# Chunk-selected attention with a gated projection on one core: half-head PSUM tiles joined to two-bank groups, one relu for both query parts, a new written order

## The chip, the cores and the metric

The kernel runs on one core of a Trainium2 chip. The metric is the device time of one execution in microseconds (us), given as the median of three runs.

## The reference, cut to what matters

There are 4 batches of 8 heads, 768 positions of 64 channels. Keys are cut into 24 chunks of 32. For every query an upper bound of each chunk's score is made from the chunk's smallest and largest key, the best 6 chunks that are not in the future are kept, and softmax attention runs over those. The result goes through a causal convolution of 5 taps, which gives a gate, and through two 512x512 projections.

```python
k_min = np.min(k_chunks, axis=3)
k_max = np.max(k_chunks, axis=3)
ub = np.sum(np.maximum(q[:, :, :, None, :] * k_min[:, :, None, :, :],
                       q[:, :, :, None, :] * k_max[:, :, None, :, :]), axis=-1)
ub = np.where(causal, ub, -1000000000.0)
top_chunks = np.argsort(ub, axis=-1)[..., -top_k:]
...
scores = np.where(mask, scale * np.matmul(q, k.transpose(0, 1, 3, 2)), -1000000000.0)
attn = softmax(scores)
x = np.matmul(attn, v)                       # heads side by side: 4 x 768 x 512
gate = 1.0 / (1.0 + np.exp(-causal_conv5(x, conv_w)))
return (gate * (x @ w_val)) @ w_out
```

## The kernel before

The 32 heads are worked as 16 pairs, 0 to 15, four pairs to a batch. `build` makes a graph of some 1500 operations, each with its engine, and `emit_in_order` writes them to the engines' queues in the order of a long list of names, `ORDER`; each engine then runs its own queue strictly in that order and waits by semaphores. So the list is what sets the order of the work, on each engine by itself. A name is an operation, a pair and a part: `E6.04` is the exponential of pair 6, head 0, score bank 4.

One pair goes through these steps:
- SP loads keys, queries and values (`Lk`, `Lq`, `Lv`). PE turns the two heads' keys into two PSUM banks (`KT`, line 649, 12 small transposes) and the queries likewise (`QT`). A bank holds, for both heads, one half of each 128-position block.
- DVE takes the largest and smallest key of each chunk, two reduces per bank, so four of 128x384 for a pair (`KX`, line 674). ACT copies the keys to fp16, one copy per bank (`KE`, line 663). POOL makes of the chunk bounds a high and a low fp16 part (`KB`, `KS`, lines 682 to 699).
- The queries, times 16, are split in the same way. ACT writes the high part QH, one copy per bank (`QH`, line 703). DVE writes the low part QL = 16 q - QH (`QL`, line 743, two of 128x320), the relu of the high part RH (`RH`, line 750, one of 128x640 fp16 from and to SBUF) and RL, the low part where q is positive and zero elsewhere (`RL`, line 756, two of 128x320: a compare of q, still in PSUM, times QL). It cannot be a relu of QL, since QH is rounded to nearest and QL can have either sign.
- PE sums the bounds with six matmuls per 128 queries (`BD`, line 784), DVE takes the 6th largest (`T8`, line 792) and marks the chunks below it (`CM`, line 799). For pairs 4 to 15 a transposing DMA on SP's queue turns the marks (`MD`).
- PE makes the scores in six groups of banks (`S`, lines 827 to 832), each group one bank for head 0 and one for head 1; the mask is added by a second matmul. A matmul of one head uses 64 of the array's rows, and those of the two heads run side by side. ACT takes the exponential, one instruction per head and bank, 128x512 or 128x128 (`E`, line 836). POOL zeroes the triangle on the diagonal (`A`, line 847). PE multiplies with the values (`AV`, line 856), DVE divides by the sum (`RC`, `NR`, lines 862 to 878).
- Per batch: the convolution as small matmuls for two pairs (`CV`, line 950) and as four multiply-adds on DVE for the other two (`TP`, line 936, "taps"), the tanh (`TH`), the value projection (`VL`, lines 964 and 971), its product with the gate, two of 128x384 per 128 channels (`GV`, line 976, DVE), the output projection (`OU`, line 984), its copy (`OE`) and the store (`ST`).

Pair 0 is handled apart, in two halves and with fp32 bounds, to start early. PE runs 36 filler matmuls (`F`, `G`, line 1002) at the start.

PSUM has 8 banks. Each group of the graph takes one bank when its first operation is written, the one that has been free for longest, and gives it back with its last:

```python
        for g in o.groups:
            if g.bank is None:
                g.bank = free.pop(0)
```

Two engines never read or write one bank at the same time: the copy on ACT and the reduces on DVE out of one bank wait for each other.

## Time and profile before

| | before |
|---|---|
| median of three runs | 175.83 us (174.57 to 175.96) |
| the profiled execution | 174.37 us, of which the span is 172.6 us and 1.77 us lie around it |
| busy in the span | PE 161.6, DVE 153.6, ACT 145.2, POOL 97.4 us |
| instructions | PE 3118 matmuls, DVE 464, ACT 320, POOL 218 |
| granted TensorE clock | 1.00 |
| first and last matmul | start 1.11 us, end 169.1 us |

In the tables of groups, "mean ns" is one instruction from its start to its end; where instructions of an engine follow each other without a pause they overlap by some tens of ns, and the chain of work gives the smaller time from one start to the next. PE's matmuls are pipelined and their ends are modelled, so that PE seems busy where it runs slowly; its real need is counted by starts.

### The profile page before, as it was taken

How to read it: one execution, taken by the hardware profiler on the slowest of the kernel's cores; microseconds unless marked ns; L12 is line 12 of the kernel's file. 1: busy time of each engine (PE TensorE's matmuls, PEld its weight loads, DVE VectorE, ACT ScalarE, POOL GpSimd, SP SyncE). 2: the span in 40 equal slices, each digit the busy share in tenths (PEclk: the TensorE clock that was granted, in tenths of full speed). 3: DMA queues.
4: the chain of work that ended last, by engine and by line, in shares of the span. 5: the costliest groups of instructions: out<-in, count | busy, mean ns of one | idle time of the engine just before them, and what ended most of it. 6: DMA issues, size and time to landing. Idle time of an engine off the chain costs nothing.

```text
span 172.6 us, 7674 instructions
## 1 busy us (share of the span) xinstructions
PE 161.6 (94%) x3118; PEld 107.8 (62%) x3118; DVE 153.6 (89%) x464; ACT 145.2 (84%) x320; POOL 97.4 (56%) x218
## 2 busy tenths in 40 slices
PE   7999999999878969999999999999999999999991
PEld 5675748776566745746764758656775646665541
DVE  0799999999999999999999999997299999669970
ACT  2387999999979988999999979797999979957441
POOL 7838489945999697186733916365718456500000
PEclk9999999999999999999999999999999999999999
DMA  4999999935999999968999979976959990334546
GB/s 95 224 240 261 235 234 251 237 75 97 193 148 220 148 211 201 213 153 198 185 183 157 237 188 217 197 158 148 233 104 238 249 217 0 66 91 181 189 187 239
DMA packets 98578, 31.50 MB, mean 182 GB/s; under 512 B 94187, under 2 KB 95467, under 8 KB 98544
## 3 DMA queue, kind: packets, MB, share of 16 engines
q1 hardware_dynamic: 97424, 29.96, 78.6%
q0 software_dynamic: 1120, 1.06, 4.2%
q8 instruction: 24, 0.39, 1.0%
q14 instruction: 10, 0.08, 0.2%
HBM read 20.98 MB, written 6.29 MB: 158 GB/s over the span
## 4 chain that ended last, share of the span: by engine, by line
PE 65%; DVE 21%; ACT 7%; POOL 2%; DMA 2%; issue 1%; DVEq 0%; POOLq 0%
PE ps L984 12%; PE ps L856 9%; PE ps L829 7%; PE ps L832 6%; PE ps L971 6%; PE ps L964 6%; ACT P L836 5%; DVE KK L674 5%; DVE G L936 5%; PE ps L649 5%; PE ps L950 4%; PE ps L784 4%; PE ps L1002 3%; DVE TOP L792 2%; DMA QM<-NS 2%; DVE QL L743 2%
## 5 line engine op out<-in xcount | busy, mean ns | idle before, releaser
L836 ACT ACTIVATE P<-ps 128x512 f16<-128x512 f32 (+1 forms) x192 | 89.6, 582 | 5.9 <-PE ps L832 5.5
L847 POOL TENSOR_SCALAR_AFFINE_SELECT P<-P 128x256 f16<-128x256 f16 (+1 forms) x64 | 37.2, 595 | 19.8 <-ACT P L836 18.4
L832 PE MATMUL ps<-QM,EM 64*128 64x512 f16 (+4 forms) x256 | 37.2, 290 | 0.7 <-DMA QM<-NS 0.4
L936 DVE SCALAR_TENSOR_TENSOR G<-xT,cwT,G 128x768 f32<-128x768 f16 x32 | 36.2, 1149 | 0.1
L674 DVE TENSOR_REDUCE KK<-ps 128x12 f32<-128x384 f32 x64 | 32.0, 546 | 4.7 <-PE ps L641 4.4
L829 PE MATMUL ps<-QH,KE 64*128 64x512 f16 (+4 forms) x256 | 35.6, 292 | 0.4 <-ACT P L836 0.4
L856 PEld LDWEIGHTS <-P 128*128 128x128 f16 x672 | 24.2, 97 | 9.0 <-issue 4.7
L856 PE MATMUL ps<-VA,P 128*128 128x65 f16 x672 | 27.5, 194 | 1.4 <-POOL P L847 1.4
L984 PE MATMUL ps<-wo,GV 128*128 128x512 f16 (+1 forms) x100 | 23.1, 371 | 0.0
L829 PEld LDWEIGHTS <-KE 64*128 64x128 f16 x256 | 13.7, 94 | 7.0 <-issue 1.4
L663 ACT ACTIVATE KE<-ps 128x384 f16<-128x384 f32 x32 | 16.1, 541 | 0.9 <-DVE KK L674 0.9
L992 ACT ACTIVATE OSB<-ps 128x512 f32<-128x512 f32 (+1 forms) x22 | 13.0, 616 | 4.3 <-PE ps L984 4.2
L976 DVE SCALAR_TENSOR_TENSOR GV<-G,ps 128x384 f16<-128x384 f32 x32 | 16.1, 542 | 0.0
L703 ACT ACTIVATE QH<-ps 128x384 f16<-128x384 f32 x32 | 15.3, 531 | 0.8 <-PE ps L829 0.6
L792 DVE MAX8 TOP<-ps 128x8 f32<-128x20 f32 (+4 forms) x160 | 15.6, 160 | 0.2
L768 POOL CAST VA<-vn 128x768 f16<-128x768 f32 x16 | 13.9, 869 | 3.2 <-DMA vn<-in_v_dram 3.1
L984 PEld LDWEIGHTS <-GV 128*128 128x128 f16 x100 | 8.7, 98 | 9.7 <-DVE GV L976 1.0
L743 DVE SCALAR_TENSOR_TENSOR QL<-ps,QH 128x320 f16<-128x320 f32 x30 | 13.8, 477 | 0.6 <-ACT QH L703 0.6
L832 PEld LDWEIGHTS <-EM 64*128 64x128 f16 x256 | 12.2, 94 | 3.4 <-issue 2.4
L756 DVE SCALAR_TENSOR_TENSOR RL<-ps,QL 128x320 f16<-128x320 f32 x30 | 13.8, 476 | 0.0
L971 PE MATMUL ps<-xT,wv 64*128 64x384 f16 x128 | 13.2, 323 | 0.4 <-DVE GV L976 0.4
L682 POOL TENSOR_TENSOR KK<-KK 128x24 f32<-128x24 f32 x15 | 3.7, 245 | 17.0 <-DVE KK L674 16.8
(87 smaller groups left out, 314.6 us busy)
## 6 DMA issues: line engine op xcount, KB each, us to landing
vn<-in_v_dram SPq DMA_DIRECT2D x16, 384.0 KB, 5.0
out_dram<-OSB SPq DMA_DIRECT2D x23, 256.0 KB, 3.4
kn<-in_k_dram SPq DMA_DIRECT2D x30, 192.0 KB, 3.9
qn<-in_q_dram SPq DMA_DIRECT2D x30, 192.0 KB, 4.1
wo<-in_moe_w_out_dram POOLq DMA_DIRECT2D x4, 128.0 KB, 4.5
kn<-in_k_dram SPq DMA_DIRECT2D x4, 96.0 KB, 2.5
qn<-in_q_dram SPq DMA_DIRECT2D x4, 96.0 KB, 2.8
wv<-in_moe_w_val_dram POOLq DMA_DIRECT2D x4, 64.0 KB, 3.7
```

What stands on the lines that cost most here:

```text
L663: nc.scalar.activation(out=spread(KE[p % 3], p, w), in_=bank(gr, None), func=AF.Copy)
L674: nc.vector.tensor_reduce(out=o, in_=i, axis=AX.X, op=ALU.min if mx else ALU.max)
L743: nc.vector.scalar_tensor_tensor(out=spread(QL[p % 2], p, w), in0=bank(gr, None)[:, 1:NT], scalar=QS, in1=spread(QH[p % 3], p, w)[:, 1:NT] ...
L792: nc.vector.max(out=TOP[p % 2][:, it - 1, s, :], in_=bank(gr, None)[:, it - 1, s * NCH:s * NCH + n])
L829: nc.tensor.matmul(out=pq[hh][:, col + a:col + n], lhsT=KE[p % 3][HP[hh], ks], rhs=QH[p % 3][HP[hh], q0 + a:q0 + n], start=True, stop=False)
L832: nc.tensor.matmul(out=pq[hh][:, col + a:col + n], lhsT=EM[HP[hh], ks], rhs=qm[HP[hh], q0 + a - 128:q0 + n - 128], start=False, stop=True)
L836: e.EX = lambda p, hh, bi, tot, gr: nc.scalar.activation(out=PT[hh, bi, p % 2][:, 0:tot], in_=bank(gr, None)[:, 0:tot], func=AF.Exp, scale ...
L847: nc.gpsimd.affine_select(out=ap, in_=ap, pattern=[[0, 2], [0, n], [1, 128]], compare_op=ALU.is_ge, fill=0.0, base=0, channel_multiplier=-1)
L856: nc.tensor.matmul(out=pav[:, qt, :], lhsT=PT[a, bi, p % 2][:, col:col + 128], rhs=VA[p % 3][:, hh, jt, :], start=(jt == 0), stop=(jt == qt))
L936: en.scalar_tensor_tensor(out=GT[sl], in0=x, scalar=w, in1=GT[sl], op0=ALU.mult, op1=ALU.add)
L971: nc.tensor.matmul(out=pv[h], lhsT=wval_sb[HP[h], gi, ws], rhs=xT[HP[h], (b % 2) * 2, gi, :, LD:LD + 128], start=(gi == 0), stop=False)
L984: nc.tensor.matmul(out=po[:, 0:z - a], lhsT=GVT[(b % 2) * NCT + et][:, s * 128:(s + 1) * 128], rhs=wout_sb[:, et, a:z], start=(et == 0), s ...
```

## The change

Four things are changed.

**Query parts.** The high part is scaled by `QD`, a little less than 16, so that its rounded value is never larger in size than 16 q; what is left, QL, then has the sign of q. High and low part lie side by side in one tile `QHL` (three of them, where QL had two buffers), and one relu of 128x1280 gives RH and RL together. The two `RL` of each pair are gone; the relu now stands behind both `QL`. The exponential's scale is divided by `QD` in place of 16.

**Two-bank groups.** A group may take two neighbouring banks (an even one and the next). The turned keys and queries, the scores of both heads, the convolution of both halves and the value projection each take such a pair of banks, and one instruction reads both: `KE`, `QH` and two `KX` per pair of heads in place of two, two and four; one `E` per score group in place of two (128x1024 or 128x256); `TH` and `GV` once per 768 columns in batches 0 to 2. In batch 3 `TH` and `GV` stay in halves. All of PSUM is one tensor of 8 banks; single banks are taken where the neighbour is already in use, if there is one.

**Nothing of PE's work changes**: the same 3118 matmuls with the same shapes.

**Written order.** `ORDER` is another list throughout.

```diff
+def take(free, size):
+    if size == 1:
+        b = next((x for x in free if x ^ 1 not in free), free[0])
+        free.remove(b)
+        return b
+    pairs = [x for x in free if x % 2 == 0 and x + 1 in free]
+    b = min(pairs, key=lambda x: max(free.index(x), free.index(x + 1)))
...
 ORDER = """
-Lk0.1 mfz F5 F14 F11 G6 mKB0 F13 cwl G11 G7 F7 F8 Lk0.0 F9 F6 ident identh G19 G2 G12 G15 KT0.1
...
+wval00 mfz F3 G12 F5 G13 G11 wval11 F12 cwl F1 F4 F2 mNS0 F15 ident mKB0 identh F6 G0 ident2 G3
...
+QD = QS * (1.0 - 2.0 ** -11)
...
-            grs = [g.group(), g.group()]
+            grs = [g.group(2)]
...
+            g.op("ACT", c, l, f"E{p}.{bi}", lambda gr=grs[0], bi=bi, tot=tot: e.EX(p, bi, tot, gr),
+                 [("sps", p, bi, hh) for hh in range(2)], keys, grs)
...
-    QH = [ct_([128, S], F16, f"QH{i}") for i in range(3)]
-    QL = [ct_([128, SELT * 128], F16, f"QL{i}") for i in range(2)]
-    RH = [ct_([128, SELT * 128], F16, f"RH{i}") for i in range(2)]
-    RL = [ct_([128, SELT * 128], F16, f"RL{i}") for i in range(2)]
+    QHL = [ct_([128, S + SELT * 128], F16, f"QHL{i}") for i in range(3)]
+    QH, QL = [x[:, 0:S] for x in QHL], [x[:, S:] for x in QHL]
+    RHL = [ct_([128, 2 * SELT * 128], F16, f"RHL{i}") for i in range(2)]
+    RH, RL = [x[:, 0:SELT * 128] for x in RHL], [x[:, SELT * 128:] for x in RHL]
...
     def RHv(p):
-        nc.vector.tensor_scalar(out=RH[p % 2], in0=QH[p % 3][:, 128:S], scalar1=0.0, scalar2=None,
+        nc.vector.tensor_scalar(out=RHL[p % 2], in0=QHL[p % 3][:, 128:], scalar1=0.0, scalar2=None,
                                 op0=ALU.max)
-    def RLv(p, w, gr):
-        nc.vector.scalar_tensor_tensor(out=spread(RL[p % 2], p, w), in0=bank(gr, None)[:, 1:NT],
-                                       scalar=0.0, in1=spread(QL[p % 2], p, w), op0=ALU.is_gt,
-                                       op1=ALU.mult)
...
-    e.EX = lambda p, hh, bi, tot, gr: nc.scalar.activation(
-        out=PT[hh, bi, p % 2][:, 0:tot], in_=bank(gr, None)[:, 0:tot], func=AF.Exp,
-        scale=0.125 / QS)
+    e.EX = lambda p, bi, tot, gr: nc.scalar.activation(
+        out=PT2[bi, p % 2][:, :, 0:tot], in_=bank(gr, None)[:, :, 0:tot], func=AF.Exp,
+        scale=0.125 / QD)
```

How the instructions stand on the engines' queues, at the three places of which the prediction speaks. The first is DVE, from the first query parts to the first marks after them. Before (`TENSOR_REDUCE` is `KX`, `COPY QM` the copy of the turned marks of pair 0, `MAX` is `T8`):

```order
L743 SCALAR_TENSOR_TENSOR QL_100<-ps_345,QH_99 128x5x64 [waits Activation_49]
L813 COPY QM_90<-ps_377 128x640 [waits PE_49]
L743 SCALAR_TENSOR_TENSOR QL_100<-ps_344,QH_99 128x5x64 [waits Activation_49]
L750 TENSOR_SCALAR RH_102<-QH_99 128x640
L756 SCALAR_TENSOR_TENSOR RL_104<-ps_345,QL_100 128x5x64 [waits DVE_49]
L743 SCALAR_TENSOR_TENSOR QL_101<-ps_389,QH_98 128x5x64 [waits Activation_49]
L750 TENSOR_SCALAR RH_103<-QH_98 128x640 [waits Activation_49]
L743 SCALAR_TENSOR_TENSOR QL_101<-ps_390,QH_98 128x5x64 [waits PE_49]
L756 SCALAR_TENSOR_TENSOR RL_104<-ps_344,QL_100 128x5x64 [waits DVE_49]
L756 SCALAR_TENSOR_TENSOR RL_105<-ps_390,QL_101 128x5x64 [waits DVE_49]
L756 SCALAR_TENSOR_TENSOR RL_105<-ps_389,QL_101 128x5x64
L674 TENSOR_REDUCE KK_109<-ps_457 128x6x2 [waits PE_49,Pool_49]
```

And in the changed kernel:

```order
L832 COPY QM_90<-psall 128x640 [waits PE_49]
L769 SCALAR_TENSOR_TENSOR QHL_99<-psall,QHL_99 128x5x64 [waits Activation_49]
L769 SCALAR_TENSOR_TENSOR QHL_99<-psall,QHL_99 128x5x64
L769 SCALAR_TENSOR_TENSOR QHL_98<-psall,QHL_98 128x5x64 [waits Activation_49]
L769 SCALAR_TENSOR_TENSOR QHL_98<-psall,QHL_98 128x5x64
L776 TENSOR_SCALAR RHL_101<-QHL_98 128x1280 [waits DVE_49]
L700 TENSOR_REDUCE KK_105<-psall 128x2x6x2 [waits PE_49,Activation_49,Pool_49]
L811 MAX TOP_113<-psall 128x8 [waits PE_49,Activation_49]
```

From the first `QL` to the next `KX` there were eleven instructions and are now five: the four `RL` are gone, the copy of the marks has moved ahead, and one of the two relus has moved behind that `KX` and the marks after it. The second place is ACT, from the end of pair 0's score groups to the second group of pair 1, with `KE` and `QH` of pair 3 in between. Before:

```order
L836 ACTIVATE P_0_121<-ps_516 128x512 [waits PE_49]
L836 ACTIVATE P_0_121<-ps_517 128x512 [waits PE_49]
L663 ACTIVATE KE_87<-ps_457 128x6x64 [waits DVE_49,Activation_49]
L703 ACTIVATE QH_97<-ps_561 128x6x64 [waits PE_49]
L703 ACTIVATE QH_97<-ps_562 128x6x64 [waits PE_49]
L663 ACTIVATE KE_87<-ps_456 128x6x64 [waits DVE_49]
L836 ACTIVATE P_1_131<-ps_606 128x128 [waits PE_49]
L836 ACTIVATE P_1_131<-ps_605 128x128
L836 ACTIVATE P_1_130<-ps_611 128x512 [waits PE_49]
L836 ACTIVATE P_1_130<-ps_612 128x512 [waits PE_49]
```

And in the changed kernel:

```order
L856 ACTIVATE P_0_116<-psall 128x1024 [waits PE_49]
L689 ACTIVATE KE_87<-psall 128x2x6x64 [waits DVE_49,PE_49,Activation_49]
L856 ACTIVATE P_0_118<-psall 128x1024 [waits PE_49]
L729 ACTIVATE QHL_97<-psall 128x2x6x64 [waits PE_49,Activation_49]
L856 ACTIVATE P_1_127<-psall 128x256 [waits PE_49]
L856 ACTIVATE P_1_123<-psall 128x1024 [waits PE_49]
```

Each two instructions on neighbouring tiles have become one of twice the size, and `KE` and `QH` stand between whole score groups. The third place is the start of POOL's queue. Before:

```order
L1015 MEMSET KB_114 128x192
L1065 DMA cwl<-in_moe_conv_w_dram 5x512
L1022 MEMSET ident 128x128
L1018 ISA
L1018 AFFINE_SELECT ident<-ident 128x128 [waits Pool_49]
```

And in the changed kernel:

```order
L1107 DMA wv_66<-in_moe_w_val_dram 32x2x512 x2
L1092 DMA cwl<-in_moe_conv_w_dram 5x512
L1042 MEMSET NS_114 128x640
L1049 MEMSET ident 128x128
L1045 ISA
L1045 AFFINE_SELECT ident<-ident 128x128 [waits Pool_49]
```

The identity matrix, without which PE's first transposes cannot run, now stands behind two weight loads and a longer memset; the memset of `KB` has moved behind it.

More of the change, by code (lines that the diff above doesn't have):

```diff
@@ L85, in emit_in_order @@
             if g.bank is None:
-                g.bank = free.pop(0)
+                g.bank = take(free, g.size)
         o.emit()
@@ L90, in emit_in_order @@
             if g.left == 0:
-                free.append(g.bank)
+                free.extend(range(g.bank, g.bank + g.size))
+def take(free, size):
[5 more added lines that the diff above has]
+    b = min(pairs, key=lambda x: max(free.index(x), free.index(x + 1)))
+    free.remove(b)
+    free.remove(b + 1)
+    return b
 PARAMS = {
@@ L209 @@
+OE3.5 ST3.5 OU3.5z OU3.1 OE3.1 OE3.5z ST3.5z ST3.1
 """.split()
@@ L310, in turn @@
                      [grs[w]])
-        kgr = [g.group(), g.group()]
+        kgr = [g.group(2)] if halves else [g.group(), g.group()]
         turn("KT", "kn", "kps", kgr, e.KT)
-        for w in range(2):
+        if halves:
+            c, l = act(S)
+            kp = [("kps", p, w) for w in range(2)]
+            g.op("ACT", c, l, f"KE{p}", lambda: e.KEv(p, None, kgr[0]), kp,
+                 [("KE", k3, w) for w in range(2)], kgr)
+            for mx in range(2):
+                c, l = dve(S)
+                g.op("DVE", c, l, f"KX{p}.{mx}", lambda mx=mx: e.KX(p, None, mx, kgr[0]), kp,
+                     [("kk", k2, mx, w) for w in range(2)], kgr)
+        for w in range(0 if halves else 2):
             gr = kgr[w]
@@ L475, in pair @@
                  [("xh", xs)], ())
-            grs = {(h, r): g.group() for h in range(2) for r in range(2)}
+            grs = {r: g.group(2) for r in range(2)}
             for a in range(2):
@@ L494, in pair @@
             for et in range(NCT):
-                grs = [g.group() for _ in range(2)]
+                grs = [g.group(2)]
                 for a, z in ((0, 1), (1, 2)):
@@ L645, in turn @@
         t = (kn if src == "kn" else qn)[p % 4]
-        po = [bank(gr, [128, NT, 64]) for gr in grs]
+        po = bank(grs[0], [128, 2, NT, 64])
         for i in range(NT):
             for h in range(2):
-                nc.tensor.transpose(out=po[h][:, i, :], in_=t[HP[h], i, :],
+                nc.tensor.transpose(out=po[:, h, i, :], in_=t[HP[h], i, :],
                                     identity=ident[HP[h], HP[h]], tile_position=(64 * h, 0))
@@ L742, in QLv @@
     def QLv(p, w, gr):
-        nc.vector.scalar_tensor_tensor(out=spread(QL[p % 2], p, w), in0=bank(gr, None)[:, 1:NT],
+        nc.vector.scalar_tensor_tensor(out=spread(QL[p % 3], p, w), in0=bank(gr, None)[:, w, 1:NT],
                                        scalar=QS, in1=spread(QH[p % 3], p, w)[:, 1:NT],
@@ L818, in SC @@
     def SC(p, bi, grs):
-        pq = [bank(gr, [128, 512]) for gr in grs]
+        pb = bank(grs[0], [128, 2, 512])
+        pq = [pb[:, hh] for hh in range(2)]
         qm = QM[p % 3].rearrange("p i c -> p (i c)")
@@ L943, in CV @@
         x = xT[:, (p // 2) % 4]
-        pc = [bank(grs[h, r], [128, HB]) for h in range(2) for r in range(2)]
+        pb = [bank(grs[r], [128, 2, HB]) for r in range(2)]
+        pc = [pb[r][:, h] for h in range(2) for r in range(2)]
         for j in range(part * KSZ, part * KSZ + KSZ):
@@ L954, with cut @@
     e.CV = CV
+    def cut(t, h):
+        return t.rearrange("p (x c) -> p x c", x=2) if h is None else t[:, h * HB:(h + 1) * HB]
     e.TH = lambda sl, h, gr: nc.scalar.activation(
-        out=GT[sl][:, h * HB:(h + 1) * HB], in_=bank(gr, None), func=AF.Tanh, scale=0.5)
+        out=cut(GT[sl], h), in_=bank(gr, None) if h is None else bank(gr, None)[:, h],
+        func=AF.Tanh, scale=0.5)
     def VL(b, et, grs, a, z):
-        pv = [bank(gr, [128, HB]) for gr in grs]
+        pb = bank(grs[0], [128, 2, HB])
+        pv = [pb[:, h] for h in range(2)]
         ws = slice(et, 256, 2) if et < 2 else slice(128 * et, 128 * et + 128)
```

289 lines of the change are left out of this document (143 added, 146 removed).

## The prediction

> **What bounds the kernel now.** I read the page's busy times first, then the stretches of the span, then the chain of work in order of time. The page's first part:
>
> ```profile
> PE 161.6 (94%) x3118; PEld 107.8 (62%) x3118; DVE 153.6 (89%) x464; ACT 145.2 (84%) x320; POOL 97.4 (56%) x218
> ```
>
> By this PE is the bound. But its ends are modelled, so I split the span where the shares change. Columns: stretch, its length, then the busy time and instructions of PE, PEld, DVE, ACT and POOL:
>
> ```profile
> 0.00:16.00 16.00, 14.41 (x136) 10.88 (x136) 10.36 (x38) 8.30 (x21) 10.83 (x30) 1.00 0.89 202
> 16.00:48.00 32.00, 29.64 (x719) 21.00 (x717) 31.72 (x118) 32.00 (x77) 24.41 (x57) 1.00 0.88 192
> 48.00:112.00 64.00, 61.32 (x1226) 41.26 (x1227) 63.59 (x189) 58.50 (x130) 39.93 (x89) 1.00 0.99 190
> 112.00:152.00 40.00, 39.16 (x780) 25.35 (x779) 33.59 (x101) 36.70 (x79) 22.19 (x44) 1.00 0.72 156
> 152.00:169.10 17.10, 17.09 (x270) 9.31 (x266) 13.90 (x21) 9.64 (x17) 0.00 (x0) 1.00 0.47 173
> ```
>
> From 16 to 112 us DVE pauses for 0.7 of 96 us. From 16 to 48 ACT pauses not at all. These two engines never wait there, so they, and not PE, set the pace; only behind 112 do both have air. The granted clock (third column from the end) is 1.00 everywhere. What PE really needs I count by starts, from pieces of the chain in which it runs without a pause (start, us, what):
>
> ```profile
> 7.39 0.65 PE ps L1002 x5
> ...
> 22.72 0.22 PE ps L829 x2
> ...
> 71.47 0.75 PE ps L784 x30
> ...
> 114.38 0.44 PE ps L649 x12
> ...
> 142.30 1.23 PE ps L856 x39
> ...
> 150.89 0.86 PE ps L984 x4
> ...
> 156.49 1.10 PE ps L950 x80
> 157.59 2.71 PE ps L971 x32
> 160.30 2.71 PE ps L964 x16
> 163.01 6.09 PE ps L984 x32
> ```
>
> One `AV` matmul takes 31.5 ns, one `BD` 25, one transpose 37, one `OU` 215, `CV` 13.8, `VL` 85 and 169, and 512 score columns of both heads 0.22 us. With the counts of the program: 672 `AV` 21.2 us, 450 `BD` 11.3, 360 transposes 13.2, 100 `OU` 21 (eight of them are half as wide), 640 `CV` 8.8, 128 and 64 `VL` 10.8 and 10.8, the scores with their mask 5120 columns a pair, 2.2 us, 35.2 for 16; the 36 fillers at 0.13 are 4.7, and some 5 remain for pair 0's own steps. That is 142 us. PE's first matmul starts at 1.1 and its last ends at 169.1: of 168 us it needs 142 and loses 26. The last 17 us lose nothing, as the pieces that follow each other there show. So the most that a relief of the other engines can give is some 20 us, and what it gives is decided from 16 to 112.
>
> **The change part by part.** PE's matmuls stay. The price of an instruction in a full queue is the step from start to start, again from the chain, with two whole groups for the slope:
>
> ```profile
> 30.55 4.03 ACT P L836 x8
> 34.58 0.38 ACT KE L663
> ...
> 43.77 0.23 DVE RH L750
> 44.00 0.40 DVE RL L756
> 44.40 0.93 DVE G L936
> ...
> 57.84 1.86 DVE KK L674 x4
> ```
>
> ```profile
> L836 ACT ACTIVATE P<-ps 128x512 f16<-128x512 f32 x160 | 84.8, 637 | 4.5 <-PE ps L832 4.2
> L836 ACT ACTIVATE P<-ps 128x128 f16<-128x128 f32 x32 | 7.8, 306 | 1.4 <-PE ps L832 1.3
> L799 DVE TENSOR_TENSOR NS<-ps,TOP 128x240 f16<-128x240 f32 x15 | 5.9, 397 | 0.3
> L799 DVE TENSOR_TENSOR NS<-ps,TOP 128x48 f16<-128x48 f32 x5 | 0.8, 201 | 0.1
> ```
>
> *RL*: each one removed is 0.40 us of DVE. *The relu*: 1280 elements in place of 640 that took 0.23. No row shows it; it costs at least 0.23 and at most twice that, 0.46. I take 0.39, nearer to the upper end since the elements double and only the start is shared: 0.16 more per pair (0 to 0.23). *`KX`*: one step is 1.86 / 4 = 0.465. The slope of the two `CM` forms is (397 - 201) / 192 = 1.02 ns per element, so 768 elements take 0.465 + 384 x 1.02 ns = 0.857, and each merging saves 0.07 (0 if the two banks cost a restart). *`GV`*, the same width from PSUM, likewise 0.07. *`E`*: a step is 4.03 / 8 = 0.504; the slope is (637 - 306) / 384 = 0.862 ns, so 1024 columns take 0.504 + 512 x 0.862 ns = 0.945 where two took 1.008: 0.063 saved (0 to 0.196, what one instruction of 637 ns has beside 512 x 0.862). *`KE`, `QH`*: 0.38 + 0.331 = 0.711 for 0.76, 0.05 saved. `TH` is the same for six instructions and stays out of the sum.
>
> The Trainium skill, "ScalarE: Activation LUTs", section "What ACT_TABLE_LOAD costs", gives 186 ns and 0.833 ns per element for such an instruction, of which some 93 ns overlap with the next. The rows agree with its slope within 4%; by it a merging saves 93 ns and the ACT term below is 3.6 in place of 2.3. I stay with the step measured here.
>
> Now by stretch. The `RL` (first two rows), the exponentials (next two) and the `GV` (last) that lie in the two full ones:
>
> ```profile
> 16.00:48.00 32.00, 5.45 (x12) 1.00 0.88 192
> 48.00:112.00 64.00, 6.53 (x14) 1.00 0.99 190
> ...
> 16.00:48.00 32.00, 24.86 (x55) 1.00 0.88 192
> 48.00:112.00 64.00, 39.28 (x85) 1.00 0.99 190
> ...
> 48.00:112.00 64.00, 7.14 (x14) 1.00 0.99 190
> ```
>
> Two `RL` are one pair, so query and key steps of six pairs lie in the first stretch and of seven in the second.
> - *16 to 48.* DVE loses 12 x 0.40 - 6 x 0.16 + 12 x 0.07 = 4.6 us. ACT loses 27 x 0.063 + 12 x 0.05 = 2.3. ACT has no pause, so it decides: **-2.3** (0 to -4.6).
> - *48 to 112.* DVE loses 14 x 0.40 - 7 x 0.16 + 14 x 0.07 + 7 x 0.07 = 6.0. ACT has 5.5 us of pause and loses 42 x 0.063 + 14 x 0.05 = 3.3, so it allows that. PE must follow: 7.5 us off in all would leave it 160 us for its 142, 89% where it now has 85%. That is what the busiest engine (DVE, 89%) reaches now, and I give it three quarters: **-4.5** (-2 to -6.5).
> - *112 to 152.* No engine but PE is near full. What counts is that `QM` and the products before it come earlier; the chain has one wait for that DMA (its row is below). I take **-1.0** (0 to -3).
> - *152 on.* PE alone, in the same order of kinds: 0.
> - *The start.* Rows of POOL, PE and the wait:
>
> ```profile
> 2.44 0.29 POOL L1018 TENSOR_SCALAR_AFFINE_SELECT ident<-ident 128x128 f32<-128x128 f32 x1
> ...
> L1080 POOL DMA_DIRECT2D wv<-in_moe_w_val_dram x4 | 2.4, 598 | 0.0
> L1015 POOL MEMSET NS<- 128x640 f16 x2 | 1.3, 636 | 0.0
> L1015 POOL MEMSET KB<- 128x192 f16 x2 | 0.5, 256 | 0.3 <-POOLq L1142 0.3
> ```
>
> ```profile
> 4.50 0.64 PE ps L641 x3
> ...
> 131.98 3.38 DMA QM<-NS
> ```
>
> The identity is ready at 2.73 now. Two weight loads (2 x 0.6) and 0.64 for 0.26 put it at 4.3; the transposes, which wait for the first keys, run from 4.3. So nothing covers a later identity, and DVE's first reduce follows the transposes at once: **+0.3** (0 to 1).
>
> Sum: -2.3 - 4.5 - 1.0 + 0.3 = **-7.5**. The profiled execution took 174.37 (span 172.6 and 1.77 around it), so 166.9 for such a one. The median of the runs shown, 175.83, stands 1.46 above it; on that footing 168.3 us.
>
> **Where a stall may go.** `KE` and `KX` read the same two banks and cannot do so together: `KE` now waits for both reduces, 2 x 0.857, where it waited for two of 0.465 on its own bank. Queued behind `KE` on ACT are the exponentials of an earlier pair, for which POOL's `A` and PE's `AV` wait. The written list puts a score group between `KX` and `KE` at the place shown, which hides it.
>
> **The rivals.**
> 1. *PE follows in full.* All of DVE's relief is taken: 30 x 0.40 - 15 x 0.16 + 30 x 0.07 + 12 x 0.07 = 12.5 us. For it: PE's last 17 us run without a loss. Against it: ACT is full from 16 to 48 and gives half as much. 161.9 for the profiled execution, 163.3 as a median.
> 2. *PE has nothing left from 48 to 112.* The chain runs through PE from 63.7 on, although DVE is full. Then only 2.3 and the start remain: -2.0, 173.8.
> 3. *The relu is held up by POOL.* It grows, and it runs while POOL is busy 56% of the span. The spread now (least, median, most ns):
>
> ```profile
> L750 DVE TENSOR_SCALAR RH<-QH x15: 283/315/866, 15.7 to 130.8; 128x640 f16<-128x640 f16 x15
> L936 DVE SCALAR_TENSOR_TENSOR G<-xT,cwT,G x32: 994/1012/2315, 44.3 to 161.1; 128x768 f32<-128x768 f16 x32
> ```
>
>    Held as the worst one was, every time, each costs 0.55 more, 7 x 0.55 = 3.9 of the 4.5: -3.6, 172.2. Against it: the median is 315. The Trainium skill, "SBUF — State Buffer", section "Who interferes with whom", says that such DVE instructions and GpSimd's share a port pair that one of them locks for its whole length; by that rule the longer relu meets more of them. The spread agrees that it happens, and how seldom.
> 4. *Slower: the banks pace.* A score group gives back its first bank after one exponential (0.504) and its second after two (1.008) now; then both after 0.945, 0.38 bank-us more, 96 times 36. The keys' banks go back after 2 x 0.465 + 0.38 and 4 x 0.465 + 0.38, 3.6 bank-us; then 2 x (2 x 0.857 + 0.711) = 4.9, 15 times 20 more. 56 over 8 banks is 7 us. If from 16 to 112 no bank is ever free, 4.1 us fall there and nothing is gained: 178.5, as a median 180. It decides from the point where PE stands before a score group because no two neighbouring banks are free while ACT and DVE have gaps; now ACT's own pauses before `E` are 5.9 us in all. That the order was written anew for pairs of banks speaks neither way, since no time is in it.
>
> **How the numbers follow.** The forecast (164 to 172) gets 0.53, rival 1 (below 164) 0.24, rival 2 0.08, rival 3 0.06, rival 4 0.09. A measurement of this kernel tells about 1% from no change, 1.76 us: the line for faster is 174.1, for slower 177.6. Rival 2 lies on the upper side of faster by a hair, so it counts half as no change; of the forecast's weight 0.07 goes there too, for all the ends of the bounds at once. Faster 0.53 - 0.07 + 0.24 + 0.04 + 0.06 = 0.80, the same 0.11, slower 0.09. The range, 162.5 to 174.5, reaches from rival 1 to the upper end of rival 2. Its sum with all bounds at their good ends (-4.6 - 6.5 - 3) is 161.7, with all at their bad ends (0 - 2 - 0 + 1) 174.8.
>
> **What would show it.** Right: DVE's busy time falls from 153.6 to some 141 and ACT's from 145 to some 137; the stretch in which DVE has no pause ends well before 112; `E` of 128x1024 steps by about 0.945 and `KX` by 0.86; PE's 142 us stand in a last-matmul end near 161.6. Wrong: ACT pausing far more than 5.9 us before `E` (rival 4), the relu's mean above 0.7 us (rival 3), or a first score matmul later than 16.5 us, which would be a start that costs more than I gave it.

## The result and the profile after

The changed kernel takes 177.52 us (176.01 to 178.38, four executions) beside 175.52 us (174.57 to 175.96, four) of the kernel before: 1.011 of its time, 95% interval 1.007 to 1.014. It is about 1% slower; 168.3 us had been forecast, in a range up to 174.5. The profiled execution took 177.8 us, of which the span is 176.1. A kernel's median below is of all its executions, its ratio only of those in the faster of the two states in which a program runs, so the two can differ by some tenths of a per cent.

The page's first part of the changed kernel, and the same stretches of its span as were read before (length, then PE, PEld, DVE, ACT, POOL, the granted clock, the DMA share, GB/s):

```profile
PE 161.0 (91%) x3118; PEld 106.7 (61%) x3118; DVE 144.5 (82%) x392; ACT 138.6 (79%) x188; POOL 101.2 (57%) x218
```

```profile
0.00:16.00 16.00, 14.06 (x116) 10.91 (x118) 8.06 (x29) 6.99 (x16) 10.35 (x28) 1.00 0.94 200
16.00:48.00 32.00, 29.17 (x719) 20.23 (x721) 29.39 (x91) 28.01 (x36) 26.08 (x62) 1.00 1.04 207
48.00:112.00 64.00, 58.62 (x1181) 39.02 (x1178) 58.30 (x158) 56.52 (x73) 40.40 (x81) 1.00 1.01 192
112.00:152.00 40.00, 38.87 (x803) 25.22 (x801) 33.33 (x94) 34.87 (x45) 23.15 (x45) 1.00 0.73 153
152.00:172.30 20.30, 20.27 (x312) 11.35 (x308) 14.72 (x24) 12.23 (x20) 1.20 (x4) 1.00 0.35 125
```

The relief came and the time did not. DVE is busy 9.1 us less and ACT 6.6 us less. The two engines that hardly paused from 16 to 48 us now do (2.6 and 4.0 of 32 us), DVE also from 48 to 112 (5.7 of 64). PE does no less, and its last matmul ends at 172.3 us where it ended at 169.1.

Where PE loses can be followed by its content. Every piece of PE's work is priced by the lower quartile of its start-to-start steps in the kernel before, which makes 142 us in all; what the time shows beyond the content started so far is the loss. Worked out so from the traces, single steps included that no view lists (us lost up to the moment; other fair prices for the pieces move a value by up to some 1.3 us, the difference of the rows by a few tenths):

| up to | 16 | 48 | 64 | 112 | 152 | last matmul |
|---|---|---|---|---|---|---|
| before | 5.3 | 12.0 | 17.0 | 22.3 | 26.6 | 27.1 |
| changed | 6.1 | 13.6 | 20.0 | 25.8 | 29.4 | 30.3 |

Of the 3.2 us 3.0 are lost before 64 us. From there to the end both lose 10 us, with DVE and ACT relieved or not.

What PE waited for, as the trace names it (line waited at, releaser: us in all, times, longest). Before:

```profile
PE ps L649 <- DVE NS L799: 1.5, 1, 1.5
PE ps L856 <- POOL P L847: 1.4, 1, 1.4
PE ps L1002 <- DVE fz L1015: 1.1, 1, 1.1
PE ps L649 <- ACT P L836: 0.5, 2, 0.3
```

And in the changed kernel:

```profile
PE psall L803 <- issue: 1.9, 1, 1.9
PE psall L803 <- DVE RHL L776: 1.7, 1, 1.7
PE psall L852 <- DMA QM<-NS: 1.5, 1, 1.5
PE psall L1029 <- DVE fz L1042: 1.1, 1, 1.1
PE psall L666 <- DMA kn<-in_k_dram: 0.8, 1, 0.8
```

This view should have been read ahead of the prediction. All of its rows before add up to 6.8 us in 11 waits, 4.6 of them released by DVE or ACT, and 1.1 of these is the memset ahead of the first matmul; 7.5 us were forecast to go. (Steps that are late by little are not listed; they make the larger part of PE's loss of 27 us, so these rows alone set no bound.) Four new rows lead the list after: the first keys, one relu, one transposed mask, and a wait that ends for no reason that the profile shows. The chain of work of the changed kernel passes through them in this order (start, us, what):

```profile
2.35 3.05 DMA kn<-in_k_dram
...
30.88 3.19 DVE RHL L776
...
49.40 1.94 issue
...
55.02 3.13 DMA QM<-NS
...
96.39 1.73 DVE KK L700 x2
```

The last of these is for the prices: two reduces in 1.73 us. The forms behind the prices, and the relu's spread (least, median, most ns):

```profile
L856 ACT ACTIVATE P<-psall 128x1024 f16<-128x1024 f32 x80 | 77.5, 1034 | 8.1 <-PE psall L852 7.5
L700 DVE TENSOR_REDUCE KK<-psall 128x24 f32<-128x768 f32 x30 | 27.6, 948 | 2.8 <-PE psall L674 1.5 <-ACT KE L689 1.1 <-ACT P L856 0.2
```

```profile
L776 DVE TENSOR_SCALAR RHL<-QHL x15: 451/483/3185, 18.4 to 134.2; 128x1280 f16<-128x1280 f16 x15
```

An exponential over both heads takes 1034 ns where two took 637 each. The relu is 483 ns in the median and 3185 once.

### The profile page after: what moved, and what is told of

Read it like the earlier page. It is cut to its first block, busy times and chain, and to the rows that moved or that the text cites. A ratio compares the mean times of both kernels' runs of the same rounds, so it can differ in the third digit from the quotient of the medians.

```text
span 176.1 us, 7491 instructions
## 1 busy us (share of the span) xinstructions
PE 161.0 (91%) x3118; PEld 106.7 (61%) x3118; DVE 144.5 (82%) x392; ACT 138.6 (79%) x188; POOL 101.2 (57%) x218
## 3 DMA queue, kind: packets, MB, share of 16 engines
q0 software_dynamic: 1120, 1.06, 4.9%
## 4 chain that ended last, share of the span: by engine, by line
PE 56%; DVE 26%; issue 6%; ACT 5%; DMA 4%; SPq 1%; DVEq 0%; ACTq 0%
PE psall L1011 11%; DVE G L957 9%; PE psall L876 8%; PE psall L849 6%; PE psall L852 5%; PE psall L803 5%; PE psall L674 4%; PE psall L972 4%; PE psall L992 4%; PE psall L999 3%; DVE KK L700 3%; DVE GV L1004 3%; ACT P L856 3%; DVE TOP L811 3%; DVE RHL L776 3%
## 5 line engine op out<-in xcount | busy, mean ns | idle before, releaser
L856 ACT ACTIVATE P<-psall 128x1024 f16<-128x1024 f32 (+1 forms) x96 | 82.9, 927 | 13.1 <-PE psall L852 12.5
L867 POOL TENSOR_SCALAR_AFFINE_SELECT P<-P 128x512 f16<-128x512 f16 (+1 forms) x64 | 36.8, 586 | 24.1 <-ACT P L856 23.3
L852 PE MATMUL psall<-QM,EM 64*128 64x512 f16 (+4 forms) x256 | 35.9, 289 | 1.6 <-DMA QM<-NS 1.5
L849 PE MATMUL psall<-QHL,KE 64*128 64x512 f16 (+4 forms) x256 | 33.4, 292 | 0.3 <-ACT KE L689 0.2
L700 DVE TENSOR_REDUCE KK<-psall 128x24 f32<-128x768 f32 (+1 forms) x34 | 29.7, 901 | 4.5 <-PE psall L666 1.7
L876 PE MATMUL psall<-VA,P 128*128 128x65 f16 x672 | 28.2, 194 | 0.7 <-issue 0.6
L1011 PE MATMUL psall<-wo,GV 128*128 128x512 f16 (+1 forms) x100 | 22.9, 370 | 0.0
L811 DVE MAX8 TOP<-psall 128x8 f32<-128x12 f32 (+4 forms) x160 | 15.6, 165 | 2.4 <-PE psall L803 1.9
L1004 DVE SCALAR_TENSOR_TENSOR GV<-G,psall 128x768 f16<-128x768 f32 (+1 forms) x20 | 15.1, 785 | 0.9 <-PE psall L992 0.7
L803 PE MATMUL psall<-KB,QHL 128*128 128x48 f16 x225 | 13.9, 183 | 1.9 <-issue 1.9
L803 PE MATMUL psall<-KB,RHL 128*128 128x48 f16 x225 | 13.9, 183 | 1.7 <-DVE RHL L776 1.7
```

The source lines that it names most:

```text
L700: nc.vector.tensor_reduce(out=o, in_=i, axis=AX.X, op=ALU.min if mx else ALU.max)
L803: nc.tensor.matmul(out=o, lhsT=lt, rhs=kb[:, j, :], start=False, stop=(n == 5), skip_group_check=True)
L811: nc.vector.max(out=TOP[p % 2][:, it - 1, s, :], in_=bank(gr, None)[:, it - 1, s * NCH:s * NCH + n])
L849: nc.tensor.matmul(out=pq[hh][:, col + a:col + n], lhsT=KE[p % 3][HP[hh], ks], rhs=QH[p % 3][HP[hh], q0 + a:q0 + n], start=True, stop=False)
L852: nc.tensor.matmul(out=pq[hh][:, col + a:col + n], lhsT=EM[HP[hh], ks], rhs=qm[HP[hh], q0 + a - 128:q0 + n - 128], start=False, stop=True)
L856: e.EX = lambda p, bi, tot, gr: nc.scalar.activation(out=PT2[bi, p % 2][:, :, 0:tot], in_=bank(gr, None)[:, :, 0:tot], func=AF.Exp, scale= ...
```

## The experiments

Ratios are to the kernel before, run beside it on the same chip, with the 95% interval.

### Query part, groups and written order taken apart

Four kernels make a square: the new query part everywhere, and of the other two changes none, one, the other, both. In the first, under the old order, `RH` stands at the place of the later `RL` of each pair (pair 2 is shown):

```diff
-QS = 16.0
+QS = 16.0
+QD = QS * (1.0 - 2.0 ** -11)
...
-... RH2 RL2.1 ... RL2.0 ...
+... RH2 ...
```

> The kernel before with the query part alone: QH by the smaller scale, QL with the sign of q, one relu over both in the place of the later of the two RL; single banks and the old written order (less two instructions per pair). Theory O (the new written order costs the time: its start, the relu that took 3.19 us, its tail; DVE's relief is worth little, since DVE is not what paces after 64 us): 174.5 to 175.5 us, at most 1 us under the kernel before. Theory G (the two-bank groups cost the time, the relief is real): about 172, the 3 to 4 us of the prediction's DVE term. Theory R (the long relu is what hurts wherever it stands): slower than before by 1 us or more, with a relu of some 3 us among its rows.

Measured: 175.18 us, 0.999 (0.995 to 1.003). DVE lost its work and nothing else happened:

```profile
PE 161.8 (94%) x3118; PEld 108.5 (63%) x3118; DVE 146.4 (85%) x434; ACT 145.2 (84%) x320; POOL 98.9 (57%) x218
```

Seven us less on DVE than before are worth nothing that can be measured. That speaks for theory O on this point, and against the prediction's largest term. Next, the new order without the groups (a few names of the list):

```diff
-... S0.5 E0.5 ... KE3 ... KX3.0 ...
+... S0.5 E0.05 E0.15 ... KE3.0 KE3.1 ... KX3.00 KX3.10 ...
```

> The new query part and the new written order, but every two-bank operation taken apart again into its two single-bank halves, one behind the other at the place of the whole. Theory O: the loss stays, 177.5 us or more (ACT and DVE have some 9 us of fixed parts back on top, so up to 180). Theory G: the loss goes with the groups, 175.5 or less. Theory R: 177.5, if the long relu is there again.

Measured: 179.85 us, 1.026 (1.019 to 1.032). The loss stays and is larger. The same wait for nothing shown (1.9 us) and the same relu (2.9 us) are there, so they belong to the order and not to the groups. And the groups without the new order:

```diff
-... S0.5 E0.05 E0.15 S0.4 E0.14 ... KE1.0 KE1.1 ...
+... S0.5 E0.5 S0.4 E0.4 ... KE1 ...
```

> All of the changed kernel's operations, two-bank groups included, under the order of the kernel before: each whole at the place of the first of its halves, some 20 instructions moved by at most four places where a buffer was not free yet. Theory O: faster than the kernel before, or equal to it: 173.5 to 175.5 us, since start, tail and the neighbours of the relu are the old ones. Theory G: the pairs of banks make PE wait here too, 177 or more. Prediction's own sum with the old order: 169 to 170.

Measured: 189.12 us, 1.079 (1.071 to 1.087). Theory O falls on this point, and so does the thought that the groups are only gain: under the old order they cost 13.9 us beside the query part alone. Of the changed kernel's longest waits none is here; there are many short ones, most of them for a bank that another engine still reads:

```profile
PE psall L672 <- ACT P L854: 1.9, 6, 0.6
PE psall L874 <- DVE NS L816: 1.6, 1, 1.6
PE psall L845 <- ACT P L854: 1.4, 4, 0.4
...
PE psall L847 <- ACT P L854: 1.2, 4, 0.3
```

All rows of this view add up to 21.5 us in 44 waits, 20.1 of them released by ACT or DVE, where the kernel before has 6.8 in 11. The square:

| | single banks | pairs of banks |
|---|---|---|
| old order | 0.999 | 1.079 |
| new order | 1.026 | 1.011, the change |

So the new order was what the groups needed (7.9% without it, a gain of 1.5% with it), and it costs 2.6% by itself. Which of the groups hurts was asked with the scores alone in pairs, under the old order:

```diff
-            grs = [g.group(), g.group()]
+            grs = [g.group(2)]
...
-... S0.5 E0.05 E0.15 ...
+... S0.5 E0.5 ...
```

> The kernel before with the new query part and one of the groups only: scores into a pair of adjacent banks and one exponential over both; K, Q, conv and value part keep single banks; old written order, each exponential at the place of the first of its halves. Theory P1 (the score pairs make the 14 us that the groups cost under the old order: 96 of them, each held until the whole exponential is through): 183 us or more. Theory P2 (the long-held pairs do, K's under three readers, the conv's and value part's): 177 or less, and faster than the kernel before if the saved fixed part of the exponentials (5 to 6 us of ACT) counts.

Measured: 202.26 us, 1.151 (1.145 to 1.156). Theory P1, and beyond it: pairs for the scores beside single banks for the rest are worse than pairs for all. Counted from the trace (each bank from its first matmul to the end of its last reader, from 16 to 152 us), the eight banks are held for 70% of the time here, 77% with all the groups under the old order, 82% in the changed kernel and 86% before. So PE stands although more banks are free. The reading, argued and not shown by a row, is that a free bank whose neighbour is taken is of no use to a score group. The list agrees: worked out by the allocator's rule, 19 of 291 groups here take a bank that was given back at most two names earlier, and 1 of 387 with the query part alone.

### Mending the single waits of the changed kernel

Four kernels mend one or more of the new long waits. First the start of the list:

```diff
-wval00 mfz F3 G12 F5 G13 G11 wval11 F12 cwl F1 F4 F2 mNS0 F15 ident mKB0 identh
+mfz F3 G12 F5 G13 G11 F12 cwl F1 F4 F2 F15 ident mKB0 identh wval00 wval11 mNS0
```

> The changed kernel with POOL's first rows alone moved: its two value-weight loads and one memset stand behind the identity matrices and not ahead of them. Theory O: the first transpose of K comes about 1 us earlier and half to all of this lasts to the end, 176.5 to 177 us. Theories G and R: the start is made up by the waits behind it, 177.5, no difference.

Measured: 177.37 us, 1.012 (1.003 to 1.020): no difference to the change's 1.011. The first scores come at 15.8 us in place of 16.8 (15.2 before), and by 64 us the time is lost again. In this profile the granted clock also fell to about half for two of the 40 slices, at 52 to 62 us, which neither of the two profiles above shows (one slice is 4.4 us, the digits are tenths of full speed, 9 is 0.9 or more). What was lost again there can be the clock's doing, so this trace doesn't tell whether the edit helped up to 64 us:

```profile
PEclk9999999999985599999999999999999999999999
```

Then all fourteen weight loads (some are shown):

```diff
-... S0.1 ... wout0 ... S2.1 ... wval10 ... S3.4 ... wvn1 Lk9.0 BD5.4 wout3 wout2 ...
+... S3.3 wval10 ... S4.0 wval11 ... S6.4 wout2 ... S6.5 wout3 ... S7.0 wout1 ...
```

> The changed kernel with its fourteen weight loads alone moved, to the places among the scores that they have in the kernel before (the first two leave the start, two of the output weights leave the first 20 us). Theory D (the new order pulls weight loads into the stretch in which the DMA engines are full anyway, 16 to 60 us, and by that the first K, a transposed mask and an instruction packet come late: 0.8, 1.5 and 1.9 us of PE's waits): 2 to 3 us go, 174.5 to 175.5. Theory N (these waits only show a loss that would come elsewhere): 177 to 177.5. The start alone gave 0.2.

Measured: 179.24 us, 1.019 (1.012 to 1.026), slower. Up to 48 us it went as theory D has it, with 11.4 us lost where the changed kernel had lost 13.6, and the wait for nothing shown is gone. Then the same loads stand in the way later:

```profile
PE psall L851 <- DMA QM<-NS: 4.1, 2, 3.2
```

So the loads do delay masks, wherever they stand; moving them as a block is no gain. The relu:

```diff
+        if p == 4:
+            nc.vector.scalar_tensor_tensor(out=RHL[p % 2], in0=QHL[p % 3][:, 128:], scalar=0.0,
+                                           in1=QHL[p % 3][:, 128:], op0=ALU.max, op1=ALU.max)
+            return
```

> The changed kernel with the one relu of pair 4, which took 3.19 us, written as a two-input maximum; nothing else. Theory L (that relu stands still while POOL's cast runs, as the one-input form alone does): it takes 1.6 to 2.0 us (1280 columns at the pace of the taps, 1.09 us for 768), and of the 1.7 us that PE waits for it 1.2 go at that place; at the end 0 to 0.7, 176.8 to 177.5, since the start run lost that wait too and gained little. Theory R (the long relu is what made the change slower): 175.5 to 176. If the two-input form takes 3 us too, the cause is not the form.

Measured: 178.95 us, 1.018 (1.012 to 1.023), and the two-input form is slower still:

```profile
L777 DVE SCALAR_TENSOR_TENSOR RHL<-QHL x1: 4140/4140/4140, 31.8 to 31.8; 128x1280 f16<-128x1280 f16 x1
```

Theory L falls: the one-input form is not what makes it long. Theory R isn't borne out either, since the start run had its relu at 1371 ns, without a wait of PE behind it, and gained nothing. And three places at once:

```diff
-    "dmam": [4, 5, 6, 7, ...],
+    "dmam": [7, ...],
...
-... MD4 ... MD5 ... MD6 ... OE3.5 ST3.5 OU3.5z OU3.1 OE3.1 OE3.5z ST3.5z ST3.1
+... MT4 ME4 ... MT5 ME5 ... MT6 ME6 ... OU3.1 OE3.1 ST3.1 OU3.5z OE3.5z ST3.5z OU3.5 OE3.5 ST3.5
```

> The changed kernel with three places mended at once: the two weight loads and the memset behind the identity matrices, the masks of pairs 4 to 6 turned on PE instead of by a DMA transpose (PE gets 0.9 us and DVE 1.3 us more work, the waits of 1.5 us for the mask go), and the last output tile's order as before. Theory W (the 1.1 per cent are these few single waits): 174.5 to 175.5, level with the kernel before. Theory S (the loss is spread and comes back elsewhere): 176.5 to 178.

Measured: 178.49 us, 1.019 (1.016 to 1.022). Theory S by the total. Which waits went can't be read here: the traced execution took 367.74 us, with PE slow from start to end (an output matmul took 800 ns in place of 370). The four long waits are where the loss shows, and none of the four edits aimed at them gave time back; three measured 0.7 to 0.8% more, of which only the last is clear of the change's own interval. The granted clock was lower too, 0.97 to 0.99 in the executions of the start and the late loads, 0.99 to 1.00 in those of the change, so a small gain can be hidden there.

Whether the loss of the new order lies before 64 us was also asked by splicing the two orders, with single banks, at pair 6:

```diff
-ORDER = old
+ORDER = old[:old.index("S6.1")] + [n for n in new if n not in old[:old.index("S6.1")]]
```

> Single banks and the new query part; the old written order up to the first scores of pair 6 (about 61 us), from there on the new written order. Beside it: the old order throughout gave 0.999 of the kernel before, the new one throughout 1.0255. Theory F (the new order loses in its first 60 us and is level from there on, as the time that PE stands behind its content has it: 16.4 against 21.3 us at 64 us, then 10.4 and 11.3 more): 1.000 to 1.008. Theory E (the loss is everywhere, or comes back later): 1.013 or more.

Measured: 179.81 us, 1.029 (1.023 to 1.035). The counterpart:

```diff
-ORDER = new
+ORDER = new[:new.index("S6.5")] + [n for n in old if n not in new[:new.index("S6.5")]]
```

> The counterpart: single banks, the new query part, the new written order up to the first scores of pair 6 (about 65 us), from there on the old one. Theory F: the loss is all there, 1.018 to 1.028. Theory E: about half, 1.008 to 1.015.

Measured: 180.37 us, 1.031 (1.025 to 1.036). The totals decide nothing, since each splice costs more than either order. In the first, one wait at the seam, for chunk bounds that POOL's new order has behind other work, takes

```profile
PE ps L773 <- POOL KB L690: 4.0, 3, 3.6
```

By content it had lost 17.4 us up to 72 us, as the old order has (17.2), 22.9 at 80, and 9.0 more to the end, where the old order loses 9.0 and the new one 8.8. That is what theory F says, in the trace alone; by its total the first splice lies where theory E had it, and the second above both theories.

### What sets the pace

Work was taken away from one engine at a time, always from the query part under the old order (0.999). From PE:

```diff
-        seq = [(RH[i2][:, ts], 0), (RH[i2][:, ts], 2), (RL[i2][:, ts], 0),
-               (QH[p % 3][:, qs], 1), (QH[p % 3][:, qs], 3), (QL[p % 3][:, ts], 1)]
+        seq = [(RH[i2][:, ts], 0), (RH[i2][:, ts], 2),
+               (QH[p % 3][:, qs], 1), (QH[p % 3][:, qs], 3)]
```

> The query part alone under the old order, as in the run before of that kind, with two of the six matmuls of each bound left out (those of the two low query parts; the bounds are then coarser and the output is not the reference's): 150 matmuls of 25 ns, 3.75 us of PE's work and nothing of DVE's or ACT's. Theory T (PE's own work sets the pace wherever it does not wait for a bank): 3 to 4 us off that run's 175.2, 171.5 to 172. Theory U (DVE and ACT set it, as the prediction had it between 16 and 112 us): at most 1 us, 174.2 or more.

Measured: 175.38 us, 1.000 (0.997 to 1.003). Theory T falls. From ACT:

```diff
-        out=PT[hh, bi, p % 2][:, 0:tot], in_=bank(gr, None)[:, 0:tot], func=AF.Exp,
+        out=PT[hh, bi, p % 2][:, 0:cutc(p, tot)], in_=bank(gr, None)[:, 0:cutc(p, tot)], func=AF.Exp,
```

> The query part alone under the old order, with 64 of the 512 columns of 140 exponentials left out from pair 2 on (the sums then use old values there and the output is not the reference's): 140 times 64 columns at 0.84 ns, 7.5 us of ACT's work and nothing of PE's or DVE's. Theory A: 171 to 173. Theory H: 174.5 or more.

Measured: 173.82 us, 0.990 (0.984 to 0.996): 7.5 us of work (ACT is busy 139.2 us in place of 145.2, so 6 of them show) give 1.4 us, which lies between the two theories. The same cut in the changed kernel:

```diff
-        out=PT2[bi, p % 2][:, :, 0:tot], in_=bank(gr, None)[:, :, 0:tot], func=AF.Exp,
+        out=PT2[bi, p % 2][:, :, 0:cutc(p, tot)], in_=bank(gr, None)[:, :, 0:cutc(p, tot)], func=AF.Exp,
```

> The changed kernel with the same 64 columns per head left out of the 70 exponentials over both heads of pair 2 and later, 7.5 us of ACT's work (output not the reference's). Theory A, carried over: ACT has slack here (119 of 136 us busy between 16 and 152), so 0 to 1 us, 176.5 to 177.5. Theory B (each pair of banks comes free only when its one exponential of 1.03 us is through, and PE's scores wait for that): 0.1 us earlier for every pair, 2 us or more at the end, 175.5 or less.

Measured: 176.78 us, 1.009 (1.006 to 1.012), as theory A carried over has it: next to nothing. Theory B, that the length of the joined exponential is what holds PE up, falls. All three engines at once, under the old order (the edits of the two runs above together):

```diff
+        seq = [(RH[i2][:, ts], 0), (RH[i2][:, ts], 2),
+               (QH[p % 3][:, qs], 1), (QH[p % 3][:, qs], 3)]
...
+        out=PT[hh, bi, p % 2][:, 0:cutc(p, tot)], in_=bank(gr, None)[:, 0:cutc(p, tot)], func=AF.Exp,
```

> The query part alone under the old order with both cuts of work at once: two of six matmuls of each bound (3.75 us of PE) and 64 of 512 columns of 140 exponentials (7.5 us of ACT) left out, on top of the 7 us that DVE has lost; the output is not the reference's. Theory H: hardly more than the cut on ACT alone gave (1.4 us): 172.5 to 174. Theory C: the three reliefs only count together, 169 to 171.

Measured: 173.69 us, 0.989 (0.984 to 0.994). Theory C falls: the reliefs do not add up to more when they come together. Besides, load off the DMA queues:

```diff
+        if what == "v" and p > 3:
+            return
```

> The run with work left out on PE, DVE and ACT at once (0.989 of the kernel before), and besides without the twelve loads of values of pairs 4 to 15 (384 KB each, 4.7 of the 31.5 MB; older values are used, the output is not the reference's). Theory M (the DMA queues set the pace from 16 to 112 us, at 185 to 193 GB/s with a share of 0.9 to 1.0): 0.975 or less, 170 or under. Theory H (the hand-over of banks in the written order does): 0.985 to 0.992.

Measured: 171.99 us, 0.979 (0.973 to 0.985), between the two theories. Beside the run with the three cuts, the DMA share fell from 1.03 to 0.81 in the middle and from 0.68 to 0.49 behind it,

```profile
48.00:112.00 64.00, 59.65 (x1153) 39.67 (x1154) 58.70 (x177) 55.68 (x133) 41.10 (x89) 0.97 0.81 150
112.00:152.00 40.00, 38.75 (x788) 25.38 (x787) 31.61 (x95) 35.16 (x81) 22.16 (x43) 1.00 0.49 114
```

and about 1% more of the time went with it. The DMA queues have a share in the pace, and they are not the pace. Last, one bank less and no work changed:

```diff
-def emit_in_order(graph, names, nbanks=8):
+def emit_in_order(graph, names, nbanks=7):
```

> The query part alone under the old order with seven banks to hand out instead of eight (eleven instructions moved by at most two places); no operation is changed. In that run's trace between 16 and 152 us the eight banks are held 900 of 1088 bank-us. Theory H (the hand-over of banks sets the pace): the same holds in seven banks would fill 900 of 952, so PE's waits for banks, 6.3 us there, at least double: 1.03 or more. Theory C (the engines together set it, each nearly full, and banks only show it): 0.99 to 1.01.

Measured: 195.23 us, 1.115 (1.111 to 1.119), 20 us. Theory C falls, and the time is far beyond theory H's bound. Between 16 and 152 us the seven banks are held 815 of 952 bank-us, 86%, as much as the eight of the kernel before. One eighth of the banks costs five times what all the reliefs together, the DMA queues' included, bring. Two other things are in this figure. The granted clock was 0.965 to 0.973, and 0.996 in the trace of the run it builds on: by an estimate at most some 6 of the 20 us (0.031 of 193.6). And the order was not made for seven banks: 21 of 387 groups now take a bank given back at most two names earlier, against 1. What an order made for seven would cost was not tried.

### Two ways to pass DVE's relief on

Since DVE had room, ACT's work was moved to it, and then to POOL, with nothing left out:

```diff
-            g.op("ACT", c, l, f"QH{p}.{w}", lambda w=w, gr=gr: e.QHv(p, w, gr),
+            g.op("DVE" if p and w else "ACT", c, l, f"QH{p}.{w}", lambda w=w, gr=gr: e.QHv(p, w, gr),
```

> The query part alone under the old order (175.2 in its own run), with one of the two copies of the high query part of each pair given from ACT to DVE: about 0.5 us each, 15 of them, so ACT loses some 7 us of work and DVE gets back what the query part had taken off it. Theory A (ACT sets the pace under the old order: in that run it stood 32.0 of 32 us busy between 16 and 48 us, and neither 7 us less on DVE nor 3.75 us less on PE moved the time): 171.5 to 173.5. Theory H (no single engine sets it, the hand-over of banks does): 174.5 to 176.

Measured: 177.58 us, 1.015 (1.010 to 1.019). DVE's copy takes 548 ns for ACT's 530; the work moved as planned and the time rose.

```diff
-    "taps": ["ACT", "DVE", "DVE", "DVE", "DVE"],
+    "taps": ["POOL", "DVE", "DVE", "DVE", "DVE"],
```

> The query part alone under the old order (0.999 of the kernel before), with the first tap of each conv slot given from ACT to POOL: 8 operations of 1.00 us leave ACT; nothing is left out. They hold no bank and read and write SBUF. Theory A (ACT's queue counts): as the cut of the exponentials, 0.985 to 0.993. Theory H (only what shortens the holding of a bank counts): 0.996 to 1.004; more if POOL's new work meets DVE's taps, which took 1.05 to 2.3 us beside a cast of POOL and 1.01 without.

Measured: 188.61 us, 1.073 (1.068 to 1.079). On POOL a tap takes 2.2 us for ACT's 1.0, and behind it in POOL's queue stand the bounds and the triangles that PE needs:

```profile
L924 POOL TENSOR_SCALAR G<-xT,cwT 128x768 f32<-128x768 f16 x8 | 17.6, 2206 | 4.7 <-DMA xT<-ON 4.5
```

```profile
PE ps L773 <- POOL KB L690: 3.1, 3, 2.5
PE ps L845 <- POOL P L836: 2.5, 2, 2.2
```

So this run doesn't tell A from H as it was meant to; whether ACT's queue counts apart from what it holds in PSUM stays open. No version with the whole computation beat the kernel before.

## Why the prediction was wrong

**The busy times were right, the step from them to time was not.** DVE was to fall to some 141 us and came to 144.5, ACT to 137 and came to 138.6. A step of `KX` is 0.865 us in the chain against 0.857. From one start to the next without a pause, worked out from the trace, the relu takes 0.40 against 0.39 and the exponential 0.90 against 0.945 (before 0.48 and not 0.504, so joining two saves 0.05). The step that failed is the first reading: "These two engines never wait there, so they, and not PE, set the pace". An engine without a pause isn't yet the one that others wait for. The runs show it: 7 us off DVE give nothing, 3.75 off PE nothing, 7.5 off ACT 1%, all together 1.1%.

**The terms, by PE's loss in each stretch** (differences of the table above):

| stretch | forecast | measured |
|---|---|---|
| start, to 16 us | +0.3 | +0.8 |
| 16 to 48 | -2.3 | +0.8 |
| 48 to 112 | -4.5 | +1.9 |
| 112 to 152 | -1.0 | -0.7 |
| from 152 on | 0 | +0.4 |
| sum | -7.5 | +3.2 |

- *48 to 112*, the largest term, failed by its premise, not by its size: three quarters of a relief that nobody waited for. Of the 1.9 us that came instead 1.4 were lost before 64 us, the wait of 1.94 at 49.4 and the mask's at 55 among them.
- *16 to 48* rested on ACT having no pause. Under the old order ACT still has none there without its own relief, and taking 7.5 us off it over the whole kernel gives 1.4. In the changed kernel it paused 4.0 us there and PE was no faster.
- *The start* was priced by the identity, which came at 4.37 us as reckoned (4.3):

```profile
4.08 0.29 POOL L1045 TENSOR_SCALAR_AFFINE_SELECT ident<-ident 128x128 f32<-128x128 f32 x1
```

  What came later still were the first keys, which landed at 5.40; the first scores came at 16.8 us, past the 16.5 that the prediction set as the mark of a costlier start.
- *The end* was taken to be free; the order of the last tiles cost 0.4.

**The rivals.** Rival 4, slower because the banks pace, had the mechanism: under the old order pairs cost 13.9 us (it had priced 4 to 7, without the banks that stand free beside a taken one). Its mark showed in the changed kernel too, where ACT's pauses before the exponential more than doubled, from 5.9 to 13.1 us, though ACT with 6.6 us less work would pause more in any case:

```profile
ACT P L856 <- PE psall L852: 12.5, 16, 1.7
```

But it isn't the whole cause. The list of names, which the prediction set aside because "no time is in it", is a plan in which every bank's next user is fixed; the new plan takes the 7.9% of the pairs away, for 2.6% of its own. Rival 2 had the time behind 64 us right: both kernels lose 10 us there, relieved or not; its relief of 2.3 us from 16 to 48 did not come. Rival 3 was right about one relu of fifteen: its mean of 697 ns stands just under the mark of 0.7 us. Mending that one relu's wait alone was not managed, and in the start run, where it went away by itself, nothing was gained, with the clock's fall in the way.

**What stays open.** Why the new order loses some 3 us before 64 us: the long waits there are where the loss shows, but four edits aimed at them left the total the same or worse, and the splices, whose seams cost as much, show the place only in the trace. Nor is the pace settled to the last: with PE, DVE, ACT and the DMA queues all relieved, 172 of 175.5 us are left. That a bank less costs 20 us shows how much hangs on the hand-over of banks under a given order; it doesn't show what would be gained by more banks, which was not tried, or by much shorter holds. Cutting the exponentials shortened holds a little, by 54 ns for each of 140 (an estimate, 64 columns at 0.84 ns); that gave 1.4 us under the old order and next to nothing in the changed kernel.

## What to carry to other kernels

Before a relief is counted as time, add up what the bound engine is recorded to wait for that engine. Here it was under 5 us, less than the gain that was forecast. This is a warning and not a bound, since most of PE's loss stood in no row; the sure way is the relief alone, everything else left as it was, as in the run with the query part under the old order. Where PSUM banks go round by a written order, the plan and the allocation are one thing: joining two banks saves a fixed part of an instruction and leaves fewer places into which a group can go, and it has to be timed with the order that was made for it and without. And mending single waits, in four tries, gave nothing back here.

## What the runs showed of the hardware

**DVE's work between SBUF tiles can be held up while POOL works.** In the changed kernel, POOL and DVE around the relu of pair 4 (start, us, engine):

```profile
30.65 0.88 POOL L787 CAST VA<-vn 128x768 f16<-128x768 f32 x1
31.50 0.40 POOL L867 TENSOR_SCALAR_AFFINE_SELECT P<-P 128x256 f16<-128x256 f16 x1
31.86 0.65 POOL L1107 DMA_DIRECT2D wv<-in_moe_w_val_dram  x1
32.52 0.84 POOL L787 CAST VA<-vn 128x768 f16<-128x768 f32 x1
```

```profile
30.88 3.19 DVE L776 TENSOR_SCALAR RHL<-QHL 128x1280 f16<-128x1280 f16 x1
```

It starts 0.23 us into a cast and ends at 34.07; up to 34.57 POOL has no pause (two more selects follow the rows shown). In the changed kernel, the other three of the square and the start run (75 relus) the five that took over 0.85 us each have a cast in them; the others took at most 0.81. It is no strict rule: in the other runs five relus of 0.92 to 1.16 us have no cast beside them but other work of POOL, and some with a cast take 0.5 to 0.65. The 64 taps of the kernels before and after, which have two inputs, take 0.98 to 1.4 us without a cast beside them, nearly all of them 1.0, and 1.06 to 2.3 with one; the two-input maximum took 4.14 beside two. The Trainium skill, "SBUF — State Buffer", section "Who interferes with whom", says that a DVE instruction with two SBUF inputs, or in a two-port mode, contends with GpSimd for a shared pair of ports. The rows agree that both forms do; that one relu can wait through several POOL instructions is more than one instruction's lock, and why is not shown.

**PE can stop in the middle of a bound's six matmuls, for nothing that the profile names.** It does so for 1.9, 1.7, 1.9 and 1.5 us in the changed kernel, the start run, the new order with single banks and the relu run, each time at the same count of PE instructions (weight loads included), some 1730, and not at all in the run with the late loads. A packet of the instruction queue starts 0.2 to 0.6 us before each, at a count of some 1720; with the late loads the same packet starts at a count of some 1595. Two more runs with this start agree: the second splice stops for 2.1 us (packet at 1724), and the changed kernel with the cut exponentials, whose packet starts at 1690, for 1.0 us only. That queue's row in the changed kernel:

```profile
q8 instruction: 24, 0.39, 1.0%
```

The Trainium skill, "Runtime: NRT & Kernel Launch", section "Instruction fetch mechanics", has instructions come in blocks of 16 KiB by the engine's own DMA queue; 0.39 MB in 24 packets agrees. That a late block is the cause is likely by this and was not tried by itself.
